# A recurrent-memory attention loop: first scores issued one key block later, and one attention result copied in two halves

## The chip, the cores and the metric

The kernel runs on one core of one Trainium2 chip. The metric is device time in microseconds (us) of one execution; lower is better. Times of the unprofiled runs are given as their median, and one further execution was taken with the hardware profiler; that one also gives the trace.

## The reference

Two independent models run side by side and their results are concatenated. Part B, a long convolution with a state-space kernel, is finished before the stretch that this document is about. Part A is an attention layer with a recurrent memory, and its passes cannot be overlapped, since each needs the memory that the one before it wrote:

```python
for s in range(n_seg):                       # 64 passes
    xs = x[:, s * seg_len:(s + 1) * seg_len, :].copy()
    h = jnp.concatenate([mem, xs], axis=1)   # 8 memory rows, 32 rows of the sequence
    q = jnp.einsum('btd,dhe->bhte', h, Wq)   # 1024 -> 32 heads of 128; k and v alike
    scores = jnp.einsum('bhqe,bhke->bhqk', q, k) * scale
    scores = jnp.where(mask[None, None], scores, -1000000000.0)
    p = _softmax(scores, axis=-1)
    o = jnp.einsum('bhqk,bhke->bhqe', p, v)
    o = jnp.einsum('bhte,hed->btd', o, Wo)
    mem = o[:, :M, :].copy()
    outs.append(o[:, M:, :])
```

All four weights are 1024 x 4096 in bf16. A pass has 40 rows, of which 32 (the memory and 24 of the sequence) depend on the recurrence; the other 8 rows of a pass are projected ahead of the loop and are read back from memory.

## The kernel before

The loop over the passes is `for s in range(NS)` in `part_a` (lines 357 to 583). The order of the instructions on each engine is the order in which the code writes them: `tc.manual_schedule()` keeps it, and the framework adds only the waits.

**Projections.** `quads` (line 358) multiplies the 32 rows by one weight block at a time. A block is 128 rows of a weight by 2048 columns, so each projection of half of the heads (`t` = 0 or 1) takes 8 blocks, numbered by `kc`. Per block there are four matmuls of 128x512, one for each group `g` of 32 columns of the TensorE array, and the four run beside each other. The matmul's line is L365. The names of the weight tiles in the profile differ (W, MF, Wlow, W_v, arena) with the place in which a block is kept.

**Streamed blocks.** Most weight blocks stay on the chip. Twelve do not fit and are read anew in every pass, 512 KB each, into four slots named wst (`stage`, line 294, DMA issue at L297 on SyncE's queue). The dictionary `STREAM` lists them: key block 2, query block 2, second key blocks 1 and 5, second query block 4, value blocks 2 and 7, second value blocks 4 and 7; `STREAM_O` adds the output blocks 4, 8 and 13. A load can be issued when the slot four loads back has been used for the last time. Three more blocks (`KEPT`) are parked in PSUM and are copied into SBUF by VectorE in each pass (`fetch`, L292); the last output block, 15, is one of them.

**First scores.** After the first keys and queries have been projected, copied out of PSUM (`evac`, L371) and transposed on TensorE (`tr`, L376), VectorE copies the transposed keys into the tile `KT0` (L489) and ScalarE the transposed queries into `QT0` (L490). The 8 rows that were projected ahead come from a tile `pk`, loaded by L327 at the end of the pass before; GpSimd puts their keys into `KT0` (`put_kl`, L379). `scores` (L390, L394) then issues 32 small matmuls into a PSUM tile `sc`. In the order of TensorE these stand in the middle of the second keys' projection, after its blocks 3, 4 and 5 and ahead of 6 and 7. After them come the softmax steps: `below` (L406, L407 on VectorE), `powers` (L410 on ScalarE), `weigh` and `turn` (L414 to L424 on VectorE).

**Second heads' result and output projection.** `pv_x` (L444, L448) multiplies the second half's values by its weights into the PSUM tile pv; `evac_o` (L460, ScalarE) copies that, 128x512, to the tile `o1`. `oproj` (L474) multiplies by the output weight, one block (two heads, eight matmuls of 32x256) at a time: blocks 0 to 4 from `o0`, then `pv_x` of the second half, blocks 5 to 7 from `o0`, and then blocks 8 to 15 from `o1`. Head `h` = 2u + hh of block `u` reads `oT[:, h % 4, ...]`: an even block reads the first two of the four slices of `o1`, an odd block the last two. While this goes on, VectorE does the softmax of 8 further rows of the second half, GpSimd builds `L1` from it (L437, L432), and VectorE fetches block 15.

**End of a pass.** Two copies (L567) take the output out of PSUM, two transposes (L573) and copies (L575) make the new memory rows of `hT`, and the next pass begins.

Of the kernel before, what the change touches and what calls it, by code (L numbers as in the profile page):

```python
# [232 lines left out]
def part_a(ctx, tc, x, src, WD, HE, seg_len, out_a, ahead, W_res, rest, places, first):  # L233
    nc = tc.nc
    S, Dm = x.shape
    M = 8
    SL = seg_len
    E = 128
    KC = Dm // 128
# [21 lines left out]
    def unit(key):  # L261
        if key in rest:

            rest.remove(key)
            load_resident(tc, wres, src, key, W_res, None, places.pop(0)() if places else None)
        if key in W_res:
            return W_res[key]
        if key in KEPT:
            return ahead_of.pop(key) + halves.get(key, [])
        between.pop(key, lambda: None)()  # L270
        if key in first:
            return first.pop(key)
        return stage(key, WD[key][:])
# [8 lines left out]
    def at(name, *dims):  # L282

        n = int(np.prod(dims))
        t_ = arena[:, AT[name] // 2:AT[name] // 2 + n]
        if len(dims) == 1:
            return t_
        names = "abc"[:len(dims)]
        return t_.rearrange("p (%s) -> p %s" % (" ".join(names), " ".join(names)), **dict(zip(names, dims)))
# [21 lines left out]
    def fetch(key):  # L311

        ahead_of[key] = []
        for name, lo, n in KEPT[key]:
            t_ = at(name, n) if name else S_[:, 0:n]
            words(t_, kept[key][lo // 1024][:, lo % 1024 // 2:(lo % 1024 + n) // 2])
            ahead_of[key].append((lo, n, t_))

    def columns(w, lo, n):

        if not isinstance(w, list):
            return [(0, w[:, lo:lo + n])]
        return [(max(lo, l_) - lo, t_[:, max(lo, l_) - l_:min(lo + n, l_ + n_) - l_]) for l_, n_, t_ in w if l_ < lo + n and lo < l_ + n_]
# [6 lines left out]
    def load_vx(j):  # L330
        n = 448 if j + 1 < NS else 256
        vx = at("vx", 448)
        nc.scalar.dma_start(out=vx[:, 0:n], in_=VXd[j + 1, :, 0:n])
        return vx
# [22 lines left out]
    for s in range(NS):  # L357
        def quads(m, t, kcs, a=None):
            if a is None:
                a = ps.tile([128, 512], F32, name="acc", tag=BANK[m, t])  # L360
            for kc in kcs:
                w = unit((m, t, kc))
                for g in range(4):
                    for o_, rhs in columns(w, 512 * g, 512):
                        nc.tensor.matmul(a[32 * g:32 * g + 32, o_:o_ + rhs.shape[1]], lhsT=hT[:, kc, :], rhs=rhs,  # L365
                                         start=(kc == 0), stop=(kc == KC - 1), tile_position=(0, 32 * g), skip_group_check=True)
            return a

        def evac(a, name):
            q = at(name, 512)  # L370
            nc.scalar.copy(out=q, in_=a[:])  # L371
            return q
# [14 lines left out]
        def scores(t, sc, QT, KT):  # L387
            for hl in range(4):
                for g in range(4):
                    nc.tensor.matmul(sc[32 * g:32 * g + SL, 0, hl, :], lhsT=QT[:, hl, g, :], rhs=KT[:, hl, g, :],  # L390
                                     start=False, stop=True, tile_position=(0, 32 * g), skip_group_check=True)
            for hl in range(4):
                for g in range(4):
                    nc.tensor.matmul(sc[32 * g:32 * g + XL, 1, hl, :], lhsT=ql[t][:, hl, g, :], rhs=KT[:, hl, g, :],  # L394
                                     start=False, stop=True, tile_position=(0, 32 * g), skip_group_check=True)
# [16 lines left out]
        def weigh(sc, i, pn):  # L412
            x, m_ = flat(sc, i), maxima(i)
            nc.vector.tensor_reduce(out=m_, in_=x, axis=AX.X, op=ALU.add)  # L414
            nc.vector.reciprocal(out=m_, in_=m_)
            pn = at(pn, x.shape[1], NK)
            nc.vector.tensor_tensor(out=pn, in0=x, in1=bc(m_.unsqueeze(2), [128, x.shape[1], NK]), op=ALU.mult)  # L417
            return pn

        def turn(pn, pt):  # L420
            n = pn.shape[1]
            pt = at(pt, n + n // 4, SL)
            nc.vector.transpose(out=pt[:, 0:n, :], in_=pn[:, :, 0:SL])
            nc.vector.transpose(out=pt[:, n:n + n // 4, :], in_=pn[:, :, SL:NK])  # L424
            return pt
# [26 lines left out]
        def pv_x(t, V, pb, lbs):  # L452

            p = ps.tile([128, 4, 128], F32, name="pv", tag="b1")
            pv(p[:], t, V, pb.rearrange("p a b c -> p a (b c)"), lbs)
            return p

        def evac_o(p, name):
            o = at(name, 4, 4, SL)
            nc.scalar.copy(out=o, in_=p[:].rearrange("p a (g q) -> p a g q", g=4))  # L460
            return o

        def pv_l(pl, t, V, L):
# [3 lines left out]
        def oproj(po, us, oT):  # L467
            for u in us:
                w = unit(("o", u))
                for hh in range(2):  # L470
                    h = 2 * u + hh
                    for qt in range(4):
                        for o_, rhs in columns(w, 1024 * hh + 256 * qt, 256):
                            nc.tensor.matmul(po[32 * qt:32 * qt + 32, o_:o_ + rhs.shape[1]], lhsT=oT[:, h % 4, (h % 16) // 4, :], rhs=rhs,  # L474
                                             start=False, stop=(h == 31), tile_position=(0, 32 * qt), skip_group_check=True)

        a = quads("k", 0, (0, 2, 4, 6, 1, 3, 5, 7))
        k0 = evac(a, "k0")
        a = quads("q", 0, range(0, 6))
# [4 lines left out]
        a = quads("k", 1, range(0, 3))  # L484
# [4 lines left out]
        nc.vector.tensor_copy(out=KT0[:, :, :, 0:SL], in_=pk_[:])  # L489
        nc.scalar.copy(out=QT0, in_=pq[:])  # L490
        vx = load_vx(s)
        quads("k", 1, range(3, 6), a)
        kl, ql = ([pk[:, 256 * t + o:256 * t + o + 128].rearrange("p (a g k) -> p a g k", a=4, g=4) for t in range(2)] for o in (0, 128))
        put_kl(KT0, 0)
        scores(0, sc0, QT0, KT0)
        quads("k", 1, range(6, KC), a)
        k1 = evac(a, "k1")
        below(sc0, None)
        powers(sc0, None)
        a = quads("q", 1, range(KC))  # L500
# [3 lines left out]
        a = quads("v", 0, range(0, 3))  # L504
# [34 lines left out]
        a = quads("v", 1, range(0, 6))  # L539
        vl = vx[:, 0:256].rearrange("p (t e) -> p t e", t=2)  # L540
        pv0 = pv_x(0, V0, pb0, lb0)
        pp = ps.tile([128, 2, 256], F32, name="pp", tag="b3")
        pv_l(pp[:, 0, 0:128].rearrange("p (a k) -> p a k", a=4), 0, V0, L0)
        o0 = evac_o(pv0, "o0")
        pt1 = turn(weigh(sc1, 0, "pn1"), "pt1")
        pb1 = at("pb1", 4, 4, SL)
# [8 lines left out]
        powers(sc1, 1)  # L555
        oproj(pp[:, 1, :], range(0, 5), o0)
        pv1 = pv_x(1, V1, pb1, [lb1])
        o1 = evac_o(pv1, "o1")
        lt1 = turn(weigh(sc1, 1, "ln1"), "lt1")
        oproj(pp[:, 1, :], range(5, 8), o0)  # L560
        L1 = left_blocks(lt1[:, 0:4, :], lt1[:, 4, :], "L1")
        fetch(("o", 15))
        oproj(pp[:, 1, :], range(8, 16), o1)
        ob = at("ob", 2, 256)
        osb = ob[:, 0, :]
        for j in range(2):
# [828 lines left out]
def kernel(  # L1395
# [92 lines left out]
    with ExitStack() as ctx_a:  # L1488
        part_a(ctx_a, tc, A_x[0], src, WD, A_Wo.shape[0] * A_Wo.shape[1], seg_len, out_a, ahead, W_res, rest, places, first)
# [35 lines left out]
```

## Time and profile before

| | |
|---|---|
| unprofiled runs, median (lowest to highest) | 2071.01 us (2070.24 to 2071.99) |
| the profiled execution's own time | 2080.33 us |
| its span in the trace | 2078.6 us |
| mean granted TensorE clock | 0.975 |
| TensorE busy (PE) | 1877.4 us, 90% |
| VectorE busy (DVE) | 1415.5 us, 68% |
| ScalarE busy (ACT) | 1047.8 us, 50% |
| GpSimd busy (POOL) | 380.1 us, 18% |
| queue q1 (the weights), share of the 16 DMA engines | 75.4% |
| data moved | 590.78 MB |

PE is TensorE's matmuls, PEld its weight loads, SP is SyncE, which only issues DMAs here. A row of the timeline or of the groups names the engine, the line, the operation, and what it writes and reads as out<-in; a count follows the x. A bracket gives the idle time of the engine ahead of the row and what ended it. A row of the waits reads: who waited, for whom, then us in total, times, and the longest in us. The span also holds the convolution and the preparation; the loop begins at about 735 us and ends at about 2017 us.

### The profile page before, as it was taken

To read this page: it belongs to the slowest core of one execution; us is meant where nothing else is said; L and a number is where in the kernel's file an instruction comes from. 1 tells how busy PE (TensorE), PEld (TensorE's weight loads), DVE (VectorE), ACT (ScalarE), POOL (GpSimd) and SP (SyncE) were. 2 spreads that over 40 slices of the span, in tenths; PEclk is the share of its full clock that TensorE was granted. 3 is DMA by queue.
4 is the path that set the end of the run, shared out by engine and by line. 5 is a ranking of instruction groups with operands and counts; after the bars stand their busy time and mean duration, and the time that the engine had idled before them with its cause. 6 is when DMAs were issued, how large, how long until landed. Compare 5 with 4: busy or idle time off the path is not lost. (4 is left out here: it accounts for less than half of the span.)

```text
span 2078.6 us, 78528 instructions
## 1 busy us (share of the span) xinstructions
PE 1877.4 (90%) x33734; PEld 1188.3 (57%) x33734; DVE 1415.5 (68%) x3352; ACT 1047.8 (50%) x1917; POOL 380.1 (18%) x748
## 2 busy tenths in 40 slices
PE   2799999977999779999999999999999999999999
PEld 1365666756888545555555555555555555555554
DVE  8689999989899346566666666656666666666650
ACT  5899999961333334444444444444444444444430
POOL 2133343452000011111111111111111111111120
PEclk8799999989999889999999999999999999999999
DMA  7697985665646999999999999999999999999991
GB/s 192 168 254 214 260 233 172 163 201 191 213 137 189 317 348 331 330 334 337 330 339 341 335 341 332 340 323 335 345 331 341 336 338 336 344 340 335 328 351 47
DMA packets 351187, 590.78 MB, mean 284 GB/s; under 512 B 108537, under 2 KB 228377, under 8 KB 348789
## 3 DMA queue, kind: packets, MB, share of 16 engines
q1 hardware_dynamic: 297016, 528.00, 75.4%
q10 hardware_dynamic: 44812, 28.26, 4.4%
q0 software_dynamic: 9008, 29.49, 4.3%
q8 instruction: 264, 4.33, 0.8%
q14 instruction: 87, 0.70, 0.1%
HBM read 530.86 MB, written 65.26 MB: 287 GB/s over the span
## 5 line engine op out<-in xcount | busy, mean ns | idle before, releaser
L365 PEld LDWEIGHTS <-a_hT 128*32 128x32 bf16 x12352 | 340.3, 96 | 294.1 <-issue 45.5
L371 ACT CAST arena<-acc 128x512 bf16<-128x512 f32 x384 | 225.1, 586 | 392.2 <-PE acc L365 333.6
L365 PE MATMUL acc<-W,a_hT 128*32 128x512 bf16 x4608 | 361.0, 382 | 0.6 <-issue 0.6
L474 PEld LDWEIGHTS <-arena 128*32 128x32 bf16 x8256 | 209.6, 96 | 110.2 <-ACT arena L460 54.7
L365 PE MATMUL acc<-wst,a_hT 128*32 128x512 bf16 x2304 | 231.9, 382 | 15.7 <-DMA wst<-WD_v 7.9
L292 DVE TENSOR_SCALAR arena<-keep 128x256 int32<-128x256 int32 (+1 forms) x512 | 176.2, 395 | 38.2 <-PE acc L365 35.1
L379 POOL COPY arena<-arena 128x128 bf16<-128x128 bf16 x128 | 37.6, 294 | 872.7 <-DMA arena<-PKd 311.4
L365 PE MATMUL acc<-MF,a_hT 128*32 128x512 bf16 x2048 | 172.5, 384 | 0.2 <-issue 0.2
L474 PE MATMUL pp<-W_o,arena 128*32 128x256 bf16 x4096 | 149.3, 275 | 5.4 <-DMA W_o<-in_A_Wo_dram 5.2
L167 PE MATMUL pro<-xTl,wsl 128*128 128x512 bf16 x512 | 123.0, 393 | 7.0 <-ACT xTl L111 4.9
L414 DVE TENSOR_REDUCE a_mx<-sc 128x4 f32<-128x160 f32 (+1 forms) x192 | 73.0, 380 | 82.4 <-ACT sc L410 82.4
L406 DVE TENSOR_REDUCE a_mx<-sc 128x4 f32<-128x160 f32 (+1 forms) x192 | 71.9, 374 | 79.5 <-PE sc L394 78.2
L1059 PEld LDWEIGHTS <-MF 128*128 128x128 bf16 x1024 | 103.1, 101 | 29.8 <-issue 8.6
L410 ACT ACTIVATE sc<-sc 128x160 f32<-128x160 f32 (+1 forms) x192 | 63.9, 333 | 108.0 <-DVE sc L407 85.1
L489 DVE COPY arena<-tr 128x512 bf16<-128x512 bf16 x64 | 27.2, 425 | 130.1 <-PE tr L376 130.1
L437 POOL TENSOR_TENSOR arena<-arena,a_BD 128x128 bf16<-128x128 bf16 x128 | 70.7, 552 | 227.7 <-DVE arena L424 204.6
L1059 PE MATMUL hps<-KT,MF 128*128 128x256 bf16 x720 | 94.7, 284 | 14.3 <-DVE x L1228 11.2
L567 ACT CAST arena<-pp 128x128 bf16<-128x128 f32 x128 | 27.7, 269 | 156.9 <-PE pp L474 156.9
L1286 PE MATMUL yp<-Bt,MI 128*128 128x256 bf16 x680 | 104.6, 274 | 0.8 <-ACT yb L1302 0.8
L1097 ACT ACTIVATE E<-pa 128x648 bf16<-128x648 f32 x128 | 91.4, 714 | 18.8 <-PE pa L1089 13.9
L460 ACT CAST arena<-pv 128x512 bf16<-128x512 f32 x128 | 75.3, 588 | 50.3 <-PE pp L444 39.7
L474 PE MATMUL pp<-wst,arena 128*32 128x256 bf16 x1536 | 77.2, 277 | 23.5 <-DMA wst<-WD_o 14.1
(313 smaller groups left out, 3976.0 us busy)
## 6 DMA issues: line engine op xcount, KB each, us to landing
wst<-WD_v SPq DMA_DIRECT2D x256, 512.0 KB
wst<-WD_k SPq DMA_DIRECT2D x192, 512.0 KB
wst<-WD_o SPq DMA_DIRECT2D x192, 512.0 KB
wst<-WD_q SPq DMA_DIRECT2D x128, 512.0 KB
Ud<-ux POOLq DMA_DIRECT2D x16, 1024.0 KB, 5.1
uq<-Ud SPq DMA_DIRECT2D x32, 512.0 KB
wsl<-in_A_Wk_dram SPq DMA_DIRECT2D x16, 512.0 KB
wsl<-in_A_Wv_dram SPq DMA_DIRECT2D x16, 512.0 KB
```

The source lines that it names most:

```text
L167: nc.tensor.matmul(a[:], lhsT=w[:, kc, 128 * j:128 * j + 128], rhs=xTl[:, kc, :, :].rearrange("p s k -> p (s k)"), start=(kc == 0), stop=( ...
L292: nc.vector.tensor_scalar(out=out.bitcast(I32), in0=in_.bitcast(I32), scalar1=0, scalar2=None, op0=ALU.bitwise_or)
L365: nc.tensor.matmul(a[32 * g:32 * g + 32, o_:o_ + rhs.shape[1]], lhsT=hT[:, kc, :], rhs=rhs, start=(kc == 0), stop=(kc == KC - 1), tile_pos ...
L371: nc.scalar.copy(out=q, in_=a[:])
L406: nc.vector.tensor_reduce(out=m_, in_=x, axis=AX.X, op=ALU.max)
L414: nc.vector.tensor_reduce(out=m_, in_=x, axis=AX.X, op=ALU.add)
L437: nc.gpsimd.tensor_tensor(out=L[:, 0].rearrange("p (a b) k -> p a b k", a=4), in0=bc(lt[:, :, 0:XL].unsqueeze(2), [128, 4, 4, XL]), in1=bc ...
L460: nc.scalar.copy(out=o, in_=p[:].rearrange("p a (g q) -> p a g q", g=4))
L474: nc.tensor.matmul(po[32 * qt:32 * qt + 32, o_:o_ + rhs.shape[1]], lhsT=oT[:, h % 4, (h % 16) // 4, :], rhs=rhs, start=False, stop=(h == 3 ...
L1059: pe.matmul(s_[r][half][:, cs, :], lhsT=MF[:, kc, 4 * rr + mc, cs, :], rhs=rhs, start=(i == 0 and mc == 0), stop=(i == 1 and mc == 3), ski ...
L1097: sc.activation(out=T["E", r, e // 4][:, lo:lo + 8 * NE].rearrange("p (i c) -> p i c", i=2), in_=T.pop(("p", r, e))[:, :, 0:4 * NE], func= ...
L1286: pe.matmul(yp[:, b, :], lhsT=m_[:, b, cs, kc, :], rhs=Bt[:, kc, j, half, c_, :], start=(kc == 0 and cs == 0 and half == 0), stop=(kc == 3 ...
```

## The change

In the second keys' projection the cut moves by one block: block 6 now comes ahead of the first scores, and only block 7 after them. `evac_o` can make its copy in parts; the second heads' result `o1` is copied as two instructions of 128x256. The eight output blocks that read it are taken in another order, the even ones first.

```diff
-        def evac_o(p, name):
-            o = at(name, 4, 4, SL)
-            nc.scalar.copy(out=o, in_=p[:].rearrange("p a (g q) -> p a g q", g=4))
+        def evac_o(p, name, parts=1):
+            o, n = at(name, 4, 4, SL), 4 // parts
+            for i in range(0, 4, n):
+                nc.scalar.copy(out=o[:, i:i + n], in_=p[:, i:i + n, :].rearrange("p a (g q) -> p a g q", g=4))
             return o
...
-        quads("k", 1, range(3, 6), a)
+        quads("k", 1, range(3, 7), a)
...
         scores(0, sc0, QT0, KT0)
-        quads("k", 1, range(6, KC), a)
+        quads("k", 1, range(7, KC), a)
...
-        o1 = evac_o(pv1, "o1")
+        o1 = evac_o(pv1, "o1", 2)
...
-        oproj(pp[:, 1, :], range(8, 16), o1)
+        oproj(pp[:, 1, :], (8, 10, 12, 14, 9, 11, 13, 15), o1)
```

## The prediction

> **What bounds the kernel now.** I read the page's slices first, for who is full in the loop.
>
> ```profile
> PE   2799999977999779999999999999999999999999
> ...
> DMA  7697985665646999999999999999999999999991
> ```
>
> From slice 15 on (the loop, 735 to 2017 us) TensorE and the 16 DMA engines are both at nine tenths. Summed over that window the trace gives TensorE 1202.3 us of 1282.0, a granted clock of 0.99 and a DMA share of 0.95 at 337 GB/s. So two things bound a pass of 20.05 us: TensorE's work with its short stalls, and the transfers close behind, idle for 0.05 x 20.05 = 1.0 us. Next the waits of TensorE and of its weight loads (700 to 2050 us), which tell what the edits can win.
>
> ```profile
> PE pp L474 <- DMA wst<-WD_o: 14.1, 20, 1.5
> PE acc L365 <- DMA wst<-WD_v: 7.9, 14, 1.8
> ...
> PE sc L390 <- POOL arena L379: 5.3, 18, 0.9
> ```
>
> ```profile
> PEld L474 <- ACT arena L460: 54.7, 120, 0.7
> ...
> PEld L390 <- ACT arena L490: 20.8, 56, 0.4
> ```
>
> Streamed blocks were late 49 times (with 12 of WD_k, 6.1 us, and 3 of WD_q, 0.7), 28.8 us in all, 0.45 us a pass. The two places that the change touches, L390 and L474, wait for ScalarE in nearly every pass. A weight load's idle time overstates what TensorE loses, so I take losses from starts in the timeline of one pass, and then from the same reading of 62 passes of the trace.
>
> **First scores.** The timeline of the pass that begins at 1497 us:
>
> ```profile
> 1502.52 0.29 POOL L379 COPY arena<-arena 128x128 bf16<-128x128 bf16 x1 [6.20 <-DMA arena<-PKd]
> 1502.60 0.59 ACT L490 COPY arena<-tr 128x512 bf16<-128x512 bf16 x1
> ...
> 1502.93 0.39 PE L365 MATMUL acc<-wst,a_hT 128*32 128x512 bf16 x4
> 1503.24 0.17 PEld L390 LDWEIGHTS <-arena 128*32 128x32 bf16 x16 [0.41 <-ACT arena L490]
> ...
> 1509.30 0.42 DVE L429 TENSOR_TENSOR arena<-arena,a_BDx 128x512 bf16<-128x512 bf16 x1 [0.39 <-PE sc L394]
> ```
>
> Two blocks of eight matmuls in all take 0.43 us elsewhere in this timeline, so one block takes 0.215. After block 5 (1502.93) TensorE was free at 1503.15; the scores began at 1503.24, just after `QT0` was complete (1503.19). Loss 0.09 us. Over 62 passes it is never under 0.09 and 0.23 on average: in 29 of them GpSimd's copy into `KT0`, which waits for the load of `pk`, ends later still (loss 0.23 to 1.09). Block 6 needs neither, and put ahead it covers up to one block in each pass. The smaller of the loss and 0.205, averaged over the passes, is **0.140 us won**. No instruction is added, and the order of streamed blocks on SyncE's queue stays.
>
> What is late next: the first softmax comes one block (0.215) closer to the second scores. VectorE's L429 waited 0.36 us for those in the typical pass (0.39 above; it needs a place that their queries hold), so 0.145 is left. But in about 10 of 62 passes VectorE has no such slack; there some 0.2 us is lost: 10/62 x 0.2 = **0.03 us given back**. ScalarE's and GpSimd's later steps on these scores have more room: `L0` is complete at 11.7 us of a pass in the median, and used at 13.7.
>
> **The copy in two halves.** The same pass:
>
> ```profile
> 1513.81 0.84 PE L474 MATMUL pp<-W_o,arena 128*32 128x256 bf16 x24
> 1513.97 0.29 ACT L410 ACTIVATE sc<-sc 128x160 f32<-128x160 f32 x1 [1.25 <-DVE sc L407]
> 1514.17 0.59 ACT L460 CAST arena<-pv 128x512 bf16<-128x512 f32 x1
> ...
> 1514.82 0.40 PE L474 MATMUL pp<-wst,arena 128*32 128x256 bf16 x8 [0.17 <-ACT arena L460]
> ```
>
> Eight of these matmuls take 0.215 us (32 take 0.97 between starts), so blocks 5 to 7 were issued by 1514.46 and TensorE lost 0.36. A ScalarE copy out of PSUM takes 586 ns for 512 columns (L460) and 269 for 128 (L567); on the line through both, 256 columns take 375. The first half then ends at 1514.55, not 1514.76: 0.21 us earlier, and blocks 8, 10, 12 and 14 need no more. The second half overlaps the first by 0.11, as L510 and L511 do, so it ends at 1514.81, while the odd blocks begin 4 x 0.215 = 0.86 us after the even ones: hidden. If the odd blocks did wait, 0.1 us would be the price. ScalarE spends 0.05 us more, and its next copy is 2.1 us away. The smaller of 0.21 and the wait for this copy, averaged over 62 passes, is 0.186. The bounds are 0 (TensorE still waits for the whole) and 0.21.
>
> The page "ScalarE: Activation LUTs", section "What ACT_TABLE_LOAD costs", gives 186 ns + 0.833 ns an element, and speaks against splitting by that fixed part. An estimate from it is 399 ns for a half and 612 for the whole; the measured whole is 586, 26 less. By it the half would save 0.187 instead of 0.211.
>
> But this gain meets another end. VectorE's chain from L429 through the second softmax to the last piece of block 15 does not move:
>
> ```profile
> 1536.53 0.21 DVE L292 TENSOR_SCALAR a_S<-keep 128x64 int32<-128x64 int32 x1
> ...
> 1536.80 0.22 PE L474 MATMUL pp<-a_S,arena 128*32 128x128 bf16 x1
> ```
>
> In the next pass (from 1517 us) this piece is complete at 1536.74 and its matmul starts 0.06 later, as fast as any wait in this trace ends: TensorE waits for VectorE there already, whatever came before. In a quarter of the passes 0.06 or less lies between the two, in the median 0.09, and 0.55 or more in the best quarter. Taking from each pass what its slack allows, 0.102 of the 0.186 is lost again: **0.084 us won**. VectorE's share of the page hides this: it is 68% busy, but from L429 to this piece it stops only for ScalarE's two exponentials (7.01 us in most passes).
>
> Block 13, streamed, moves one block back. It is used 0.215 later in the order and its slot is freed as much later, about what the first half wins, so the load behind it (second key block 5) is issued at the same time as before, with the longest time of all until its use. In the first pass the loads of resident output blocks change order with their use: 0, at most 2 us once.
>
> **What the transfers take back.** Sum of a pass: 0.140 - 0.030 + 0.084 = 0.194 us; times 64, 12.4 us. A streamed block has the time from its slot's release until its use four loads later, a third of a pass. A pass shorter by 0.194 takes 0.065 from each of 12. 49 of 768 uses waited already; they alone wait 12 x 0.064 x 0.065 = 0.05 longer, and blocks that were just in time come on top. Another reading: over the 62 passes, one that lost 1 us more to anything but a transfer was itself 0.48 us longer, 0.64 +- 0.23 with the next one counted. I take 0.6: **7.5 us** kept. The bounds are 0 and all.
>
> The page "HBM Reference", "Specifications (TRN2)", says that a core streaming alone reaches about 425 GB/s. By that the 6.67 MB of a pass would take an estimated 15.7 us, nothing would be taken back, and the sum would be 12.4 us. The measured share of 0.95 at 337 GB/s speaks against it, and I go by the row.
>
> The profiled execution took 2080.33 us (span 2078.6, 1.7 around it): 2080.3 - 7.5 = 2072.8. The unprofiled median is 9.3 lower; the same step from there gives **2063.5**.
>
> **Rivals.**
> - *Nothing is taken back.* For: the transfers idle 1.0 us a pass. Against: 49 late blocks, and VectorE's chain. Gain from 12.4 (the sum above) to (0.140 + 0.186) x 64 = 20.9 if that chain did not bind either: 2050 to 2059. Chance 0.13.
> - *The transfers are the bound, or the half copy is not waited for alone.* Then waits for wst replace those removed. For: DMA nine tenths in every slice. Gain 0 to 4: 2069. Chance 0.20.
> - *Slower: the first softmax is late.* Place: L429, behind the first heads' steps on VectorE. It decides from the 0.145 us that are left. If VectorE overruns by a block in all passes, the 7.0 us chain behind it ends 0.215 later, at block 15's last piece, where TensorE has no slack: 64 x 0.215 = 13.8 us lost against 0.6 x 0.14 x 64 = 5.4 won: 2079. Against: a slack of 0.36 in most passes. Chance 0.09.
>
> **How the numbers follow.** The forecast case (gain 4.2 to 12) has 0.58. Faster by over 0.2% (4.1 us, about what a measurement of this kernel can tell from no change): 0.58 + 0.13 = 0.71; within, 0.20; slower, 0.09. The range 2053 to 2070 takes in the forecast case, half of the first rival and most of the second.
>
> **What the profile after would show.** Scores: PEld L390's wait for L490 gone, POOL L379's mostly gone; DVE L429's wait at 0.15. Copy: a wait for L460 shorter by 0.2, two copies near 375 ns. Taken back: `a_S` matmuls 0.06 after their copy in most passes, and more than 29 us of waits for wst. I am wrong if those stay at 29 (then more is kept), or if L429 no longer waits.

## The result, and the profile after

The changed kernel is 0.43% faster: ratio to the kernel before 0.9957, 95% interval 0.9942 to 0.9972, from 22 runs of each (medians 2067.26 and 2077.07 us). On a time of 2077 us that is 8.9 us, 5.8 to 12.0. The kernel before has a wider spread than its first three runs showed (2068.09 to 2091.69), so the difference is read from the ratio and not from single times. The profiled execution of the changed kernel took 2060.34 us (span 2058.6), 20 us less than the profiled one of before. Of that, 4.5 us lie ahead of the end of the first pass (753.5 and 749.0 us), and 15.6 in the 62 passes after it, where the ratio has 8.9: a single execution scatters by several us, and so do the readings of a single trace.

The same rows of the page's slices:

```profile
PE   2699999977999779999999999999999999999999
...
DMA  7697986565736899999999999999999999999991
```

Both are still at nine tenths through the loop: these rows do not show the change. It is seen in the waits. Those of TensorE, 700 to 2050 us (L475 is the old L474, L461 the old L460, L491 the old L490):

```profile
PE acc L365 <- DMA wst<-WD_v: 10.0, 16, 2.0
PE pp L475 <- DMA wst<-WD_o: 6.7, 13, 0.8
...
PE pp L475 <- ACT arena L461: 1.0, 4, 0.3
PE sc L390 <- POOL arena L379: 0.6, 2, 0.4
```

where the kernel before had, for the copy,

```profile
PE pp L474 <- ACT arena L460: 7.6, 36, 0.3
```

and those of its weight loads:

```profile
PEld L475 <- ACT arena L461: 39.1, 96, 0.8
...
PEld L390 <- ACT arena L491: 10.4, 55, 0.2
```

The wait ahead of L390 fell from 20.8 to 10.4 us, and that for the copy from 54.7 to 39.1. TensorE's own wait for the copy fell from 7.6 us to 1.0, and the one for GpSimd's copy into `KT0` from 5.3 to 0.6. Waits for the streamed output blocks fell from 14.1 to 6.7 us (9.4 in a second profile of the changed kernel), and all waits for wst from 28.8 to 24.7 (28.0 in the second).

The timeline of a pass of the changed kernel, around the first scores and then around the copy:

```profile
1489.99 0.59 ACT L491 COPY arena<-tr 128x512 bf16<-128x512 bf16 x1 [0.36 <-PE tr L376]
1490.32 0.39 PE L365 MATMUL acc<-wst,a_hT 128*32 128x512 bf16 x4
1490.51 0.29 POOL L379 COPY arena<-arena 128x128 bf16<-128x128 bf16 x1 [6.66 <-DMA arena<-PKd]
1490.54 0.39 PE L365 MATMUL acc<-W,a_hT 128*32 128x512 bf16 x4
...
1490.85 0.28 PE L390 MATMUL sc<-arena 128*32 128x40 bf16 x16
...
1495.41 0.49 DVE L432 TENSOR_TENSOR a_S<-arena,a_BDL 128x128 bf16<-128x128 bf16 x1
...
1496.04 0.43 DVE L429 TENSOR_TENSOR arena<-arena,a_BDx 128x512 bf16<-128x512 bf16 x1
```

```profile
1500.36 0.84 PE L475 MATMUL pp<-W_o,arena 128*32 128x256 bf16 x24
1500.57 0.29 ACT L410 ACTIVATE sc<-sc 128x160 f32<-128x160 f32 x1 [1.29 <-DVE sc L407]
1500.77 0.65 ACT L461 CAST arena<-pv 128x256 bf16<-128x256 f32 x2
...
1501.20 0.40 PE L475 MATMUL pp<-wst,arena 128*32 128x256 bf16 x8
...
1502.86 0.21 DVE L292 TENSOR_SCALAR a_S<-keep 128x64 int32<-128x64 int32 x1
...
1503.12 0.22 PE L475 MATMUL pp<-a_S,arena 128*32 128x128 bf16 x1
```

`QT0` is complete at 1490.58, while block 6, begun at 1490.54, runs until 1490.75. Only GpSimd's copy (until 1490.80), late through the load of `pk`, still delays the scores by 0.1 us. VectorE has 0.14 us left ahead of L429 (1495.90 to 1496.04) where it had 0.39. Blocks 5 to 7 are issued by 1501.01, and the first block on `o1` starts at 1501.20: a loss of 0.19 where it was 0.36. The last piece of block 15 is complete at 1503.07 and its matmul starts 0.05 later: here TensorE waits for VectorE.

The same readings over 62 passes of each trace, in us a pass. "Again" is a second profile of the changed kernel, from the experiment after_again:

| | before | after | again |
|---|---|---|---|
| loss ahead of the first scores, mean | 0.228 | 0.098 | 0.112 |
| loss ahead of the first block on o1, mean | 0.347 | 0.145 | 0.135 |
| VectorE's slack ahead of L429, median | 0.36 | 0.15 | 0.15 |
| passes in which the last piece of block 15 is complete under 0.07 ahead of its use | 27 | 40 | 37 |
| first score matmul minus transposes (tr0), mean | 1.490 | 1.555 | 1.594 |
| from there to the second transposes, mean | 3.232 | 3.057 | 3.072 |
| from block 5's first matmul to block 15's last, mean | 2.910 | 2.733 | 2.741 |
| whole pass, mean | 20.047 | 19.795 | 19.807 |
| streamed blocks of the projections late, mean | 0.348 | 0.469 | 0.445 |
| streamed output blocks late, mean | 0.216 | 0.118 | 0.117 |

The last two rows go by starts. For each of the 425 matmuls of a pass, the time since the start of the matmul ahead of it is compared with the median of the same place in all 62 passes of that trace, and what the matmuls on wst have above it is added up. The list of waits shows less, since it counts from the end of a matmul: that comes 0.38 us after its start, while the next block can start after 0.215.

### The profile page after: what moved, and what is told of

The parts are those of the page before. It is cut to its first block, busy times and chain, and to the rows that moved or that the text cites. A ratio compares the mean times of both kernels' runs of the same rounds, so it can differ in the third digit from the quotient of the medians.

```text
span 2058.6 us, 78592 instructions
## 1 busy us (share of the span) xinstructions
PE 1875.7 (91%) x33734; PEld 1190.4 (58%) x33734; DVE 1416.1 (69%) x3352; ACT 1051.5 (51%) x1981; POOL 379.8 (18%) x748
## 4 chain that ended last, share of the span: by engine, by line
PE 35%; DMA 17%; DVE 1%; issue 1%; ACT 1%; POOL 0%; ACTq 0%; POOLq 0%; DVEq 0%
PE acc L365 20%; PE pp L475 7%; DMA wst<-WD_v 4%; DMA wst<-WD_o 4%; DMA wst<-WD_q 3%; PE pe L611 3%; DMA wst<-WD_k 3%; DMA arena<-PKd 2%; PE tr L376 2%; PE pv L444 1%; DMA out_dram<-arena 1%; PE sc L390 1%; PE pv L448 1%; ACT arena L568 0%; PE sc L394 0%
## 5 line engine op out<-in xcount | busy, mean ns | idle before, releaser
L365 PE MATMUL acc<-W,a_hT 128*32 128x512 bf16 x4608 | 375.8, 383 | 0.8 <-issue 0.7
L475 PEld LDWEIGHTS <-arena 128*32 128x32 bf16 x8256 | 212.1, 97 | 93.9 <-issue 45.3
L475 PE MATMUL pp<-W_o,arena 128*32 128x256 bf16 x4096 | 138.2, 275 | 7.7 <-DMA W_o<-in_A_Wo_dram 6.3
L490 DVE COPY arena<-tr 128x512 bf16<-128x512 bf16 x64 | 27.2, 425 | 130.7 <-PE tr L376 130.7
L461 ACT CAST arena<-pv 128x256 bf16<-128x256 f32 (+1 forms) x192 | 79.1, 449 | 49.0 <-PE pp L444 39.1
L365 PE MATMUL acc<-W_v,a_hT 128*32 128x512 bf16 x1280 | 93.7, 382 | 0.9 <-issue 0.8
```

The lines of the kernel that those rows point to most:

```text
L461: nc.scalar.copy(out=o[:, i:i + n], in_=p[:, i:i + n, :].rearrange("p a (g q) -> p a g q", g=4))
```

## The experiments

Where a time is given as a ratio it stands against runs of the kernel before on the same chip, with its 95% interval.

**The scores alone.**

```diff
-        quads("k", 1, range(3, 6), a)
+        quads("k", 1, range(3, 7), a)
...
-        quads("k", 1, range(6, KC), a)
+        quads("k", 1, range(7, KC), a)
```

> Only the first scores are moved behind block 6. My theory (TensorE's losses go, VectorE's chain from L429 to the last piece of block 15 caps the second edit, and the transfers take back about 0.4 of what is left): 0.110 us a pass raw, some 4 us faster than before (2 to 7). Rival A, the transfers are the bound and TensorE's losses hardly count: under 2 us. Rival B, the transfers take nothing back: 7 to 9 us. The loss ahead of L390 falls from 0.23 to about 0.10 us a pass, VectorE's wait ahead of L429 from 0.36 to 0.15.

Measured: 0.9986 (0.9970 to 1.0003), 2.9 us faster, in an interval from 6.2 faster to 0.6 slower. The loss ahead of L390 was 0.073 us a pass and VectorE's slack at L429 0.15, as foreseen. The size fits my theory (4 us) better than the rival of nothing taken back (7 to 9), which lies outside of the interval, but it does not exclude that the transfers take nearly all.

**The copy and the block order alone**, that is, the changed kernel with the scores in their old place.

> Only the copy in two halves with the even blocks first. My theory: 0.084 us a pass raw, some 3 us faster (1 to 6), because in half of the passes the matmul of block 15's last piece then waits for VectorE. Rival A, the transfers are the bound: under 2 us. A rival in which VectorE's chain does not matter and the transfers take nothing: 0.186 x 64 = 12 us. The loss ahead of the first block on o1 falls from 0.35 to about 0.15 us a pass in each.

Measured: 0.9990 (0.9968 to 1.0012), 2.1 us faster, in an interval from 6.6 faster to 2.5 slower. The loss ahead of the first block on `o1` was 0.166 us. A gain of 12 us is excluded; 3 us and 0 are not told apart. The two halves of the change add up to 5.0 us, both together gave 8.9; the intervals overlap.

**Block 15's last pieces on ScalarE.** `fetch` copies the three pieces of output block 15 in the order Oa, Ob, and the short one in `S_`:

```diff
-            words(t_, kept[key][lo // 1024][:, lo % 1024 // 2:(lo % 1024 + n) // 2])
+            part = kept[key][lo // 1024][:, lo % 1024 // 2:(lo % 1024 + n) // 2]
+            if key == ("o", 15) and name != "Oa":
+                nc.scalar.copy(out=t_, in_=part.bitcast(BF16))
+            else:
+                words(t_, part)
```

> The changed kernel, with the last two pieces of output block 15 copied by ScalarE, which is idle there, in place of VectorE. My theory: VectorE's chain ends 0.5 us earlier, the 0.10 us a pass that it took back are won, some 4 us more than the changed kernel's 9: 11 to 16 us faster than before. Rival A, the transfers take back whatever is won: no more than 1 us beyond the changed kernel's 9.

Measured: 1.0007 (0.9988 to 1.0026): some 10 us slower than the changed kernel. The expectation failed because the edit puts in a wait that I had not seen:

```profile
1512.77 0.38 DVE L292 TENSOR_SCALAR arena<-keep 128x256 int32<-128x256 int32 x1
...
1513.26 0.48 ACT L318 COPY arena<-keep 128x384 bf16<-128x384 bf16 x1 [1.36 <-DVE arena L292]
...
1513.63 0.27 ACT L318 COPY a_S<-keep 128x128 bf16<-128x128 bf16 x1
...
1513.79 0.27 PE L479 MATMUL pp<-arena 128*32 128x256 bf16 x2 [0.19 <-ACT arena L318]
```

ScalarE was idle for 1.36 us and began when VectorE's piece was done: both read the same PSUM tile, and the framework lets the second reader wait for the first. The page "PSUM — Partial Sum Buffer" of the Trainium skill, section "PSUM bank collisions raise a hardware error", says that two engines may not read one bank in the same partitions at the same moment, which may be why; the run shows the wait alone. So this kernel became another experiment: a delay in front of block 15. Its stretch from block 5 to the last matmul took 3.017 us on average, against 2.733 and 2.741: 0.28 x 64 = 17.9 us put in, 10.4 us (5 to 15) come out, **0.58** of it (0.3 to 0.9).

**The halves in the old block order.**

```diff
-        oproj(pp[:, 1, :], (8, 10, 12, 14, 9, 11, 13, 15), o1)
+        oproj(pp[:, 1, :], range(8, 16), o1)
```

> The changed kernel with the output blocks 8 to 15 in the old order: the second block already needs the second half of the copy. My theory: the first half is waited for alone, block 9 then waits some 0.06 us for the second half, and VectorE's chain hides that in most passes: within 2 us of the changed kernel (7 to 9 us faster than before). Rival, the even blocks first are what wins: no better than the scores moved alone.

Measured: 0.9983 (0.9965 to 1.0001), 5.6 us (1 to 10) behind the changed kernel's 0.9956 (its two sets of runs). I had expected less than 2, and the rival's sign holds: no better than the scores alone. The second half of the copy is not enough to explain it: block 9 waits for it 0.04 us in the median pass and 0.02 on average, 1.5 us in all, and the median stretch from block 5 to the last matmul stays the same (2.757 us), since VectorE's chain hides it. What grew in the waits is a streamed block:

```profile
PE pp L475 <- DMA wst<-WD_o: 13.8, 21, 1.3
```

In the new order block 13 is used one block later. Its average lateness is 0.054, 0.089 (the changed kernel twice), 0.056, 0.074, 0.064 and 0.073 us a pass in the six profiles of full kernels that have the new order, and 0.133, 0.087 and 0.158 in the three with the old one: 0.06 us a pass, 3.7 us, that I had put at nothing. This is the likely reason and not a shown one. The two groups touch (0.089 and 0.087), and in this trace block 8 was later too (0.207 us against 0.145 and 0.135), though its place in the order is the same.

**The pieces on ScalarE, mended.** To e3's edit this adds that the two pieces go to ScalarE ahead of VectorE's piece in the order of the program:

```diff
-        for name, lo, n in KEPT[key]:
+        for name, lo, n in sorted(KEPT[key], key=lambda piece: key == ("o", 15) and piece[0] == "Oa"):
...
+        ahead_of[key].sort(key=lambda piece: piece[0])
```

> The changed kernel with the last two pieces of block 15 copied by ScalarE ahead of VectorE's first piece (the two read one PSUM bank, and the framework orders them; in e3_block15_scalar ScalarE had to wait for VectorE). Theory 1, VectorE's chain caps the second edit: its end moves from 0.05 us ahead of the use to some 0.5 us ahead, and 0.10 us a pass or more is won: 3 to 8 us beyond the changed kernel, 0.9915 to 0.994 of before. Theory 2, the transfers take back whatever is won: the same as the changed kernel, 0.9957.

Measured: 0.9968 (0.9941 to 0.9995). The chain did get shorter (VectorE's own piece is complete 0.22 us ahead of its matmul in the median pass and 0.08 at the least; 0.5 was expected), and the stretch from block 5 on took 2.647 us instead of 2.733. The time did not fall below that of the changed kernel (0.9957).

**Three streamed blocks fewer**, for the kernel before, the changed one and e5. The weights of a resident block stand in for those of three streamed ones, so this kernel leaves out three loads a pass; its other instructions are the same.

```diff
+LIGHT = {("v", 0, 2): ("v", 0, 1), ("v", 1, 4): ("v", 1, 3), ("o", 8): ("o", 7)}
...
+        if key in LIGHT:
+            return W_res[LIGHT[key]]
         return stage(key, WD[key][:])
```

> The kernel before with three streamed blocks fewer in each pass: value block 2, second value block 4 and output block 8 take a resident block's weights instead (so a part of the sums uses wrong weights). Transfers fall by a quarter, to some 0.72 of the DMA engines. Both theories: waits for wst near 0, 0.45 us a pass, 28 us faster than before; less if VectorE's chain holds the passes up.

> The changed kernel with the same three streamed blocks fewer. Against l_before: theory 1 (VectorE's chain is what caps the second edit, and without late blocks it does so in every pass) some 0.06 to 0.12 us a pass, 4 to 8 us. Theory 2 (the transfers took the difference back): the whole 0.33 us a pass, 18 to 21 us.

> The kernel of e5_scalar_pieces_first with the same three streamed blocks fewer. Against l_after: theory 1, with no transfers to wait for, the chain's whole cost comes free: 0.12 to 0.2 us a pass, 8 to 13 us. Theory 2: the chain costs nothing, 0 to 2 us.

Measured: 0.9767 (0.9731 to 0.9803), 0.9737 (0.9697 to 0.9777) and 0.9695 (0.9661 to 0.9729); medians 2024.0, 2017.9 and 2010.5 us. The change is worth 6.1 us here and e5 7.4 more (runs of l_e5 2004.2 to 2012.1, of l_after 2013.0 to 2026.9; l_before, 2019.8 to 2029.9, overlaps with l_after). For the change that is within the 4 to 8 us expected; for e5 it is a little under the 8 to 13. The kernel before gained 48 us (41 to 56) where 28 were expected, although the DMA share fell to 0.80 and not to 0.72. TensorE waited for wst once in l_before and four times in l_after. Without late blocks the passes are alike, so the medians of the stages show the terms by themselves:

| us a pass, median | l_before | l_after | l_e5 |
|---|---|---|---|
| loss ahead of the first scores | 0.088 | 0.001 | 0.001 |
| loss ahead of the first block on o1 | 0.386 | 0.174 | 0.173 |
| first scores minus tr0, and on to the second transposes | 1.295 + 3.154 | 1.424 + 2.942 | 1.424 + 2.942 |
| block 5 to block 15's last matmul | 2.765 | 2.758 | 2.552 |
| from the left rows' matmul (pl) to the transposes at the end of the pass | 0.472 | 0.425 | 0.472 |
| whole pass | 19.138 | 18.995 | 18.840 |

The scores bring 0.083 in this state. The copy takes 0.21 off its wait, and the stretch behind it is shorter by 0.007: VectorE's chain has it all. The last piece in l_after, and the same piece, from ScalarE, in l_e5:

```profile
1480.89 0.21 DVE L295 TENSOR_SCALAR a_S<-keep 128x64 int32<-128x64 int32 x1
...
1481.15 0.22 PE L478 MATMUL pp<-a_S,arena 128*32 128x128 bf16 x1
```

```profile
1483.61 0.29 ACT L321 COPY a_S<-keep 128x128 bf16<-128x128 bf16 x1
...
1484.22 0.38 DVE L295 TENSOR_SCALAR arena<-keep 128x256 int32<-128x256 int32 x1
...
1484.84 0.22 PE L483 MATMUL pp<-a_S,arena 128*32 128x128 bf16 x1
```

0.05 us between the two in the first, as in all 62 passes of it; 0.94 in the second. With VectorE's chain out of the way the copy's 0.21 comes through (2.758 to 2.552).

**The changed kernel and e5 once more, on one chip, and both with one streamed block fewer** (only value block 2).

> The changed kernel unchanged, on the chip of the next run and beside it: 0.9957 of before, 0.994 to 0.9975 under every theory. It is the base for the next.

> The kernel of e5_scalar_pieces_first unchanged, on the same chip as after_again. If VectorE's chain is worth 0.6 of 0.1 us a pass in the full kernel: 4 us faster than after_again. If the transfers take all of it back, as the first run of it suggests: within 2 us of after_again.

> The changed kernel with one streamed block fewer in each pass (value block 2 takes a resident block's weights, so a part of the sums is wrong). Transfers at some 0.9 of the DMA engines. If the transfers cost in proportion, a third of what three fewer saved, 16 to 17 us less than the changed kernel; if the cost is that of standing near the full rate, more than half of it, 25 to 35 us less.

> The kernel of e5_scalar_pieces_first with the same one streamed block fewer. Against m_after: if it is the transfers that take back what e5 wins, relief of one block lets most of it through, 4 to 7 us; if something else does (a cost of e5's own on ScalarE), no more than 1 us.

Measured: 0.9955 (0.9933 to 0.9978), 0.9969 (0.9947 to 0.9992), 0.9865 (0.9833 to 0.9897) and 0.9870 (0.9838 to 0.9901). In the full kernel e5 is again not ahead of the changed one: 2.9 us behind here, 2.3 in the first runs (each some 6.5 us either way), where my theory had it 4 ahead. One block fewer saves 19 us, three save 46, each some 8 or 9 us either way: in proportion as far as that shows, with the DMA share at 0.91. Even there e5 wins nothing (+1.0 us, an interval of some 9 us either way), though its stretch from block 5 on is 0.19 us shorter on average (2.640 against 2.830) in a pass of nearly the same mean length (within 0.04). In the trace m_e5's longer stages are those with streamed blocks, the first projection (4.496 against 4.397) and the value blocks ahead of the second scores (1.924 against 1.867), with equal medians. That speaks for transfers that come later by what was won. The waits that the profile puts down to wst hardly show it (11.8 us in m_after, 13.0 in m_e5), but by starts the streamed blocks were late by 0.25 us a pass in m_after and by 0.36 in m_e5: 0.11 of the 0.19 came back there. Two profiles of one kernel can differ by as much (0.73 and 0.58 in the two of e5), so this stays in part open: the local gain is shown, that it is not seen in the time is shown within some us, and the transfers as the taker are shown by the light kernels, in which it is not lost, and only hinted at by these starts.

## Why the prediction was right

It gave 7.5 us, with 2053 to 2070 us for the median; measured are 8.9 us (5.8 to 12.0) and 2067.3. The median is 3.8 us above the forecast 2063.5 although the gain is larger, because the kernel before has 2077.1 over 22 runs and not the 2071.0 that the step was taken from. That the gain is so close is in part luck: more was won in the pass than the sum had, and less of it was kept, as far as these readings go. Step by step:

- **First scores, 0.140 us a pass.** Right: the loss fell by 0.130 and 0.116, and by 0.087 of 0.088 in the light kernels, where `pk` is hardly ever late (the loss is 0.001 in the median and on average in l_after). In two of the 62 passes of before, the loss was 0.00 and 0.01 and not at least 0.09: block 5 itself came late there. The weight loads' wait for L490 was to vanish and only halved, but TensorE is still at work on block 6 during what is left of it.
- **What is late next, VectorE at L429.** The slack left was 0.146 in the median for a predicted 0.145. The 0.03 given back was counted too high: in the trace of before VectorE's slack is under 0.215 in five of 62 passes and not in ten, and after the change it is under 0.05 in four, as it was before.
- **The copy, 0.186.** Right: 378 ns for a half (375), and the loss fell by 0.202 and 0.212.
- **VectorE's chain takes 0.102 of that.** The mechanism is shown by l_after against l_e5. It bound in 27 passes before and in 40 and 37 after. In the full kernel the stretch became 0.17 us shorter, more than the 0.084 foreseen; 0.06 of that is block 13.
- **Block 13, put at 0.** This is the term that was mis-sized. I reckoned when its slot is freed, and did not count that the block itself was late in 16 of 62 passes and now has one block's time more. One of these stood in the prediction's own working: the "32 take 0.97" has 0.10 us of waiting for block 13 in it, and the same 32 take 0.87 in the next pass of the trace (1535.32 to 1536.19). It may be worth about 3.7 us before the transfers' share.
- **What the transfers take back, 0.4.** e3's delay went through at 0.58, for 0.6. Summed from the traces, the losses that went (0.130 + 0.202 + 0.06) less what VectorE's chain adds (0.10 at the two last matmuls) are 0.29 us a pass, 18.7 us; 8.9 of it (5.8 to 12.0) are 0.48, in a range from 0.31 to 0.64. The 0.29 comes from one trace of before, in which the pass itself shortened by 0.25, more than the 0.14 of the ratio; so the share is rough, and rougher than this range. I had foreseen more than 29 us of waits for wst; they were 24.7 and 28.0 in the window of the prediction, so this sign failed. By starts, the streamed blocks of the projections did come later, by 0.348 us a pass before and 0.469 and 0.445 after: some 0.1 us, 7 us in all, returned there. The six other profiles of full kernels also lie above 0.348 (0.38 to 0.63), but there is only one trace of before, and the two traces of e5 differ by 0.18.

The three rivals: that nothing is taken back (12.4 us and more) lies just outside of the interval, which ends at 12.0, and e1 and e3 speak against it too. That the transfers are the bound is half true: three loads fewer save 46 us where the waits for wst were 28.8 in all. By starts the late blocks of before come to 0.56 us a pass, 35 us, and the lateness of `pk` adds to that. Slower through L429 did not come, since its slack was not used up.

Of the two places of the Trainium skill that the prediction weighed, "ScalarE: Activation LUTs", section "What ACT_TABLE_LOAD costs", gives an estimate of 399 ns for a half copy, where 378 were measured in the median. "HBM Reference", section "Specifications (TRN2)", has about 425 GB/s for a core that streams alone; a load fewer would then be worth nothing, and it saved 19 us at a rate of 341 GB/s.

No version beat the changed kernel in the full program; e5 is level with it at best.

## What to carry to other kernels

A wait that is taken away is worth what the next one in line allows: follow each edit to the point where its gain meets another engine's chain, and measure the slack there over all passes and not in one, because a chain on an engine that is 68% busy can still be what ends last. When weights are streamed through a few slots, an order of use is also a deadline for each load: moving the one load that is most often late behind resident work may be worth as much as the wait that the reorder was made for. In this kernel, with the DMA engines 95% busy, about half of what was won or put in elsewhere came through (0.48 and 0.58, both with wide ranges); try a gain that vanishes again with fewer transfers before it is called unreal.

## What the runs showed of the hardware

- A matmul that starts behind a stall is followed sooner by its reader. ScalarE's first output copy starts 0.25 us after block 15's last matmul in the changed kernel (1503.12 to 1503.37 in the trace), where TensorE stood still ahead of that matmul, and 0.31 in the kernel before and 0.30 in l_e5, where it had not or hardly. Over the 62 passes of the changed kernel's trace it is 0.25 in the median of the 38 passes with a stall and 0.30 in that of the 24 without; in l_after, with a stall in every pass, 0.25. This fits the 0.047 us between 0.472 and 0.425 in the table of the light kernels: so much of the wait for VectorE comes back at once. Why the matmul's end comes sooner, the runs do not show.
- The time of a pass followed the number of streamed blocks about in proportion, 19 us for one and 46 for three out of twelve (each some 8 or 9 us either way), down to a DMA share of 0.80. Both are more than a like share of the 28.8 us of waits that the list names.
